# First 16 attention units: value product with queries on partitions, and x divided by the sums of its rows

## The chip, the cores and the metric

The kernel runs on one core of a Trainium2 chip. The metric is the device time of one execution in microseconds. A second source is the profile of one execution: a trace of every instruction of the five engines (PE is TensorE with its weight loads PEld, DVE is VectorE, ACT is ScalarE, POOL is GpSimd, SP is SyncE, which issues the transfers here), read as rows of several views.

## The reference

Attention with a bias from a running sum, then two feed-forward layers:

```
scores = q @ k.T / 8 + min(-(cum_i - cum_j), 0)     # causal, cum = cumsum(max(s, 0)); B=4, H=8, S=576, D=64
attn   = exp(scores - max) ; attn = attn / (sum(attn) + 1e-9)
x      = (attn @ v), heads side by side             # 2304 x 512
x      = (sigmoid(x @ w_gate) * (x @ w_val)) @ w_out  # 512 -> 1536 -> 512
h      = x @ w_in ; out = (h - tanh(h)) @ w_out2      # 512 -> 2048 -> 512
```

All inputs are fp32.

## The kernel before

Attention runs over 64 units, each one head of one batch with a group of queries: first the 256 leading queries (G = 0) of every batch and head, then the other 320 (G = 1). A unit of G = 0 has two steps, one for each tile of 128 queries (128 and 256 keys). The first N32 = 16 units (batches 0 and 1, steps 0 to 31) work in plain fp32; later ones split every operand in a high and a low part. The change is about these first 32 steps.

One loop over the steps writes the order of all engines out by hand; each engine works its instructions off in that order. In step i the loop issues, for the first 16 units:

- DVE: `ttr(i)`, the scaled scores and their minimum out of PSUM; then, for step i - 2, `eps` (adds 1e-9 to the row sum) and `recip`; `norm(i - 2)`, which multiplies the 128 x 128 or 128 x 256 tile of exponentials by the reciprocal, on POOL, from unit 13 on (steps 26 to 31) on DVE.
- ACT: `evac(i - 3)` (copies transposed probabilities out of PSUM), then `exp(i)` with the row sum as accumulator output.
- PE: the scores of step i + 2 (`qk`), a gate or value product of the feed-forward layer where there is one (`moe`, 12 matmuls of 256 columns) or, in the first 20 steps, a few warming products, then the transposes of step i - 2 (`tr`), then, every second step, a value product (`pv`), then a further gate or value product where two are due.
- the evacuation of the value product one step later (`xsum`): ACT writes the high part of x, and DVE the low part another step later (list `late`).

The value product has v of two heads as its stationary operand (128 columns: two heads of 64) and the transposed probabilities as the moving one, so x comes out with the head dimension on partitions, as the feed-forward layer wants it; of the two heads in the result only the unit's own half is read. Transposes go to PSUM banks 6 and 2 in turn for the first 16 steps, then to bank 6; the value product goes to bank 7; the gate products use banks 0 to 2, the scores 3 to 5.

When the last head of a batch has been written to x (`whole`), its 24 gate and value products are put into a queue `mq`. Each step takes as many as keep pace with the steps that are left:

```
k = -(-len(mq) // left) if i < n else 1
left -= 1
for mm in mq[:k]:
    cvt.finish(min(2 * mm[1] + mm[2] + AHEAD, len(cq) - 1))
```

The weights of these products come as 64-bit words and are turned into high and low fp32 parts on the way, 24 jobs in all. A tick of this conversion is one instruction on ACT (`words_scale`, L78), two on DVE for the job before (`words_join`, L82 and L83), and ACT's high part (L124) and POOL's low part (L114) for the job before that. There is a tick every third step up to step 15, one in each step from 18 on, and further ones where a product would come before its weights (`cvt.finish`).

Transfers are all issued by SP in the order of the loop: q and k of a unit four units ahead (`load_kq`, five buffers), its row of running sums (`load_sum`), v of a pair of heads two units ahead (`load_vc`, four buffers), weights by the conversion. A transfer whose buffer isn't free holds up those behind it.

Of the kernel before, what the change touches and what calls it, by code (L numbers as in the profile page):

```python
# [8 lines left out]
F = mybir.dt.float32  # L9
# [3 lines left out]
AF = mybir.ActivationFunctionType  # L13
ALU = mybir.AluOpType

B, H, S, D = 4, 8, 576, 64
# [14 lines left out]
NK = 4  # L31
# [6 lines left out]
N32 = 16  # L38
AHEAD = 1
TR2 = 16  # L40
# [18 lines left out]
def NORM(G, t):  # L59
    return "pool" if t > 2 else "dve"  # L60
# [3 lines left out]
def attention_moe_moe2(ctx: ExitStack, tc: tile.TileContext, kqT, v, s, wg, wv, wo, win, wo2, out):  # L64
# [8 lines left out]
    def bank(i, shape):  # L73
        return psum.tile(shape, F, tag=f"bank{i}", name=f"bank{i}")
# [205 lines left out]
    def load_vc(u):  # L280
        if u >= len(units):
            return
        b, h, q0, kw, qw, nj = shape(u)
        d = U_[u]
        if u < N32:
            if h % 2:
                d["v"] = U_[u - 1]["v"]
            else:
                d["v"] = at.tile([128, 2, 2, D], F, tag="kl", name="vpair", bufs=NK)
                for a in range(2):  # L290
                    SP.dma_start(out=d["v"][:, :, a], in_=v[b, h + a, :, 0:nj])
            return
        load_c(u)
        load_v(u)
# [138 lines left out]

    def exp(i):
        e = T_[i]
        e["sum"] = sm.tile([128, 1], F, tag="sum", name="sum")
        ACT.activation(out=e["sp"], in_=e["sp"], func=AF.Exp, scale=-1.0, bias=e["m"], accum_out=e["sum"])  # L437

    def eps(i):
        if 0 <= i < n:  # L440
            DVE.tensor_scalar(out=T_[i]["sum"], in0=T_[i]["sum"], scalar1=1e-9, scalar2=None, op0=ALU.add)

    def recip(i):
        if 0 <= i < n:
            T_[i]["r"] = sm.tile([128, 1], F, tag="r", name="r")
            DVE.reciprocal(out=T_[i]["r"], in_=T_[i]["sum"])

    def norm(i):
        if 0 <= i < n:
            e = T_[i]  # L450
            u, t = steps[i]
            if u < N32 - 3 or NORM(units[u][1], t) == "pool":
                POOL.tensor_scalar(out=e["sp"], in0=e["sp"], scalar1=e["r"], scalar2=1.0, op0=ALU.mult, op1=ALU.mult)  # L453
            else:
                DVE.tensor_scalar(out=e["sp"], in0=e["sp"], scalar1=e["r"], scalar2=None, op0=ALU.mult)

    def tr(i):
        if i < 0 or i >= len(steps):
            return
        u, t = steps[i]  # L460
        e = T_[i]
        blocks = [128 * j for j in range(t + 1)] if t < 4 else [0, 128, 256, 384, 448]
        ps = bank(2 if i < TR2 and i % 2 else 6, [128, min(len(blocks), 4), 128])
        e["tr"] = [ps]
        if t == 4:
            e["tr"].append(bank(3 + nqk[0] % 3, [128, 1, 128]))
            nqk[0] += 1
        for j, c in enumerate(blocks):
            PE.transpose(e["tr"][j // 4][:, j % 4, :], e["sp"][:, c:c + 128], ident)  # L469
# [24 lines left out]
        DVE.tensor_tensor(out=pl[:, js, o:o + 128], in0=tr0, in1=ph[:, js, o:o + 128].bitcast(F), op=ALU.subtract)  # L494

    X_ = {}
    late = []

    def pv(u):
        b, G, h = units[u]  # L500
        q0, qw, ts = GRP[G]
        d = U_.pop(u)
        ps = bank(7, [128, qw])
        if u < N32:
            for j in range(2):
                PE.matmul(ps[:, j * 128:], d["v"][:, j].rearrange("p a d -> p (a d)"),
                          d["p"][:, 2 * j:2].rearrange("p s q -> p (s q)") if j == 0 else d["p"][:, 2],
                          start=(j == 0), stop=(j == 1))
            return ps
        ph, pl = (P_[x][:, u % 2] for x in range(2))  # L510
        jobs = [(0, 0, 0), (1, 3, 0)] if G == 0 else [(0, 0, 0), (1, 1, 0), (2, 2, 0), (3, 3, 64), (4, 4, 64)]
        for n, (j, slot, o) in enumerate(jobs):
            for m, p in enumerate((ph, pl)):
                PE.matmul(ps[:, o:qw], d["vs"][:, j].rearrange("p a d -> p (a d)"), p[:, slot, o:qw],  # L514
                          start=(n == 0 and m == 0), stop=(n == len(jobs) - 1 and m == 1))
        return ps

    def xsum(u, ps):
        b, G, h = units[u]
        q0, qw, ts = GRP[G]  # L520
        g = 2 * b + G
        if h == 0:
            X_[g] = [xt.tile([128, KD, 320], R, tag=f"x{p}", name=f"x{p}")[:, :, :qw] for p in "hl"]
        a = 64 * (h % 2)
        if u < N32:
            xh, xl = (x[a:a + 64, h // 2, :] for x in X_[g])
            ACT.activation(out=xh, in_=ps[a:a + 64], func=AF.Copy)

            def rest():
                DVE.tensor_tensor(out=xl, in0=ps[a:a + 64], in1=xh.bitcast(F), op=ALU.subtract)  # L530

            if h == H - 1:
                rest()
            else:
                late.append(rest)
            return
        if h % 2 == 0:
            X_["pair"] = at.tile([128, 320], F, tag="xp", name="xp", bufs=1)[:, :qw]
        xp = X_["pair"]
        ACT.activation(out=xp[a:a + 64], in_=ps[64 - a:128 - a], func=AF.Copy)  # L540
        DVE.tensor_tensor(out=xp[a:a + 64], in0=ps[a:a + 64], in1=xp[a:a + 64], op=ALU.add)

    def xsplit(u):
        b, G, h = units[u]
        g = 2 * b + G
        if u >= N32 and h % 2:
            xp = X_["pair"]
            xh, xl = X_[g]
            ACT.activation(out=xh[:, h // 2, :], in_=xp, func=AF.Copy)
            POOL.tensor_tensor(out=xl[:, h // 2, :], in0=xp, in1=xh[:, h // 2, :].bitcast(F), op=ALU.subtract)  # L550
# [44 lines left out]
    SP.dma_start(out=sraw, in_=s.rearrange("b h s -> (b h) s"))  # L595
    kq32 = [ld.tile([65, 512], F, tag="kq", name=f"kq32{j}") for j in range(2)]
    kq32 += [at.tile([65, 512], F, tag="kh", name=f"kq32{j + 2}", bufs=NK) for j in range(NK - 1)]
    cvt = Conversion(cv, cq, 3, 3, 1, pt, 2, late=2, cut=2)
    for u in range(2):
        load_kq(u)  # L600
# [22 lines left out]
        DVE.tensor_tensor_scan(out=cum[:, c], data0=sraw[:, c], data1=zt[:, c], initial=init, op0=ALU.add, op1=ALU.add)  # L623
    load_sum(0)
    load_sum(1)
    for kq in ones[2:]:
        DVE.memset(kq, 1.0)
    cvt.load(2)
    load_vc(0)
# [19 lines left out]
    mq = []  # L649
    n = len(steps)  # L650
    lag = [2 if j < 2 * N32 else LN for j in range(n)]
    xq, xs, pvs = [], [], []

    def whole(xu):
        if units[xu][2] == H - 1 and xu < len(units) - 1:
            gg = 2 * units[xu][0] + units[xu][1]
            mq.extend((gg, m, w) for m in range(M1) for w in range(2))

    for i in range(n + LN + 2):
# [18 lines left out]
            recip(j)  # L678
            norm(j)
        cvt.low()  # L680
        while late:
            late.pop(0)()
        for e in es:
            evac(e)
        if i < n:
# [10 lines left out]
        while xq:  # L696
            xu, ps = xq.pop(0)
            xsum(xu, ps)
            if xu < N32:
                whole(xu)  # L700
            else:
                xs.append(xu)
        if first and vparts:
            vparts.pop(0)()
# [34 lines left out]
            warm(4 if i < 4 else 1)  # L739
        for j in js:  # L740
            tr(j)
        for e in es:
            if steps[e][1] in (1, 4):
                pvs.extend(range(steps[e][0] - steps[e][1] // 4, steps[e][0] + 1))
# [327 lines left out]
```

## Time and profile before

| | |
|---|---|
| time, median of 3 runs | 1058.3 us (1056.79 to 1058.71) |
| the profiled execution | 1059.05 us |
| its span, first to last instruction | 1057.3 us |
| PE busy | 1024.0 us, 97% |
| DVE, ACT, POOL busy | 629.3, 512.6, 457.3 us |
| mean granted clock of PE | 0.993 |
| steps 0 to 31 | from 7.6 to 92.0 us of the span |

The profiled execution is 0.75 us above the median. Times in the rows below count from the first instruction of the profiled execution. Where a row ends in square brackets, they hold how long the engine stood idle before it and what released it; the releaser is inferred.

### The profile page before, as it was taken

How to read it: one execution, taken by the hardware profiler on the slowest of the kernel's cores; microseconds unless marked ns; L12 is line 12 of the kernel's file. 1: busy time of each engine (PE TensorE's matmuls, PEld its weight loads, DVE VectorE, ACT ScalarE, POOL GpSimd, SP SyncE). 2: the span in 40 equal slices, each digit the busy share in tenths (PEclk: the TensorE clock that was granted, in tenths of full speed). 3: DMA queues.
4: the chain of work that ended last, by engine and by line, in shares of the span. 5: the costliest groups of instructions: out<-in, count | busy, mean ns of one | idle time of the engine just before them, and what ended most of it. 6: DMA issues, size and time to landing. Idle time of an engine off the chain costs nothing.

```text
span 1057.3 us, 19634 instructions
## 1 busy us (share of the span) xinstructions
PE 1024.0 (97%) x6812; PEld 952.9 (90%) x6812; DVE 629.3 (60%) x1467; ACT 512.6 (48%) x1178; POOL 457.3 (43%) x608
## 2 busy tenths in 40 slices
PE   6888999999999999999999999999999999999998
PEld 5687999999999999999988888988888889999997
DVE  5688565677576476644523544265755245877876
ACT  5776465677566566644423333244453233334333
POOL 3677454666557466623300100046555202454442
PEclk8999999999999999999999999999999999999999
DMA  6674456756565456316453332355687686444433
GB/s 190 215 238 126 116 139 166 205 148 181 154 176 171 135 180 185 111 43 220 159 166 112 119 119 77 116 177 204 233 294 288 244 311 237 147 114 140 140 98 103
DMA packets 109091, 177.09 MB, mean 167 GB/s; under 512 B 16000, under 2 KB 71296, under 8 KB 107712
## 3 DMA queue, kind: packets, MB, share of 16 engines
q1 hardware_dynamic: 108992, 175.85, 53.4%
q8 instruction: 53, 0.87, 0.3%
q14 instruction: 46, 0.38, 0.1%
HBM read 128.79 MB, written 47.00 MB: 166 GB/s over the span
## 4 chain that ended last, share of the span: by engine, by line
PE 83%; DMA 4%; POOL 3%; DVE 3%; ACT 3%; issue 3%; SPq 1%; POOLq 0%; DVEq 0%; ACTq 0%
PE bank L572 8%; PE bank L576 8%; PE bank L573 8%; PE bank L886 6%; PE bank L885 6%; PE bank L889 6%; PE bank L1025 5%; PE bank L1024 5%; PE bank L1023 5%; PE bank L847 5%; PE bank L843 5%; PE bank L844 5%; PE bank L514 4%; PE bank L469 4%; PE bank L410 1%
## 5 line engine op out<-in xcount | busy, mean ns | idle before, releaser
L1025 PE MATMUL bank<-wo,sl 128*128 128x256 f32 x504 | 142.9, 284 | 1.4 <-DVE sl L934 1.4
L1023 PE MATMUL bank<-wo,sh 128*128 128x256 f32 x504 | 141.7, 281 | 0.0
L1024 PE MATMUL bank<-wo,sh 128*128 128x256 f32 x504 | 141.7, 281 | 0.0
L886 PE MATMUL bank<-y,ring 128*128 128x512 f32 (+1 forms) x320 | 115.8, 368 | 0.0
L885 PE MATMUL bank<-y,ring 128*128 128x512 f32 (+1 forms) x320 | 115.7, 368 | 0.0
L892 DVE TENSOR_TENSOR th<-bank,th 128x512 f32<-128x512 f32 (+1 forms) x80 | 50.1, 635 | 92.3 <-ACT th L891 90.2
L114 POOL TENSOR_TENSOR ring<-tmp,ring 128x512 fp32r<-128x512 f32 x16 | 22.6, 1413 | 186.9 <-ACT ring L124 166.7
L493 ACT ACTIVATE pth<-bank 128x384 fp32r<-128x384 f32 (+1 forms) x96 | 45.4, 473 | 118.7 <-PE bank L469 93.2
L1025 PEld LDWEIGHTS bank<-wo,sl 128*128 128x128 f32 x504 | 95.2, 189 | 3.0 <-DVE sl L934 2.0
L929 POOL TENSOR_TENSOR s<-g 128x256 f32<-128x256 f32 (+1 forms) x40 | 36.9, 922 | 139.8 <-DMA g<-h 131.0
L494 DVE TENSOR_TENSOR ptl<-bank,pth 128x384 fp32r<-128x384 f32 (+1 forms) x96 | 51.2, 534 | 75.2 <-ACT pth L493 63.1
L1023 PEld LDWEIGHTS bank<-wo,sh 128*128 128x128 f32 x504 | 95.2, 189 | 0.0
L1024 PEld LDWEIGHTS bank<-wo,sh 128*128 128x128 f32 x504 | 95.2, 189 | 0.0
L800 DVE TENSOR_TENSOR gl<-g,gh 128x512 fp32r<-128x512 f32 (+1 forms) x60 | 37.8, 637 | 84.1 <-PE bank L847 62.5
L437 ACT ACTIVATE sp<-sp,nm 128x128 f32<-128x128 f32 (+4 forms) x144 | 83.5, 580 | 7.6 <-DVE nm L430 7.6
L469 PE MATMUL bank<-ident,sp 128*128 128x128 f32 x400 | 69.1, 277 | 16.8 <-POOL sp L453 6.6
L891 ACT ACTIVATE th<-bank 128x512 f32<-128x512 f32 (+1 forms) x80 | 43.5, 550 | 78.4 <-PE bank L889 75.8
L889 PE MATMUL bank<-y,ring 128*128 128x512 f32 (+1 forms) x320 | 78.7, 368 | 0.0
L799 ACT ACTIVATE gh<-g 128x512 fp32r<-128x512 f32 (+1 forms) x60 | 35.1, 591 | 90.0 <-PE bank L844 82.4
L588 DVE SCALAR_TENSOR_TENSOR gt<-th,bank 128x256 f32<-128x256 f32 (+1 forms) x96 | 43.2, 450 | 56.4 <-PE bank L576 41.9
L341 POOL TENSOR_TENSOR kl<-kq,kh 128x576 fp32r<-128x576 f32 (+1 forms) x48 | 57.7, 1203 | 38.9 <-ACT kh L340 38.5
L932 ACT ACTIVATE sh<-g 128x768 fp32r<-128x768 f32 (+1 forms) x40 | 31.2, 781 | 87.6 <-PE bank L1024 60.7
(385 smaller groups left out, 3181.3 us busy)
## 6 DMA issues: line engine op xcount, KB each, us to landing
h<-th SPq DMA_DIRECT2D x64, 256.0 KB, 2.7
kq<-in_kq SPq DMA_DIRECT2D x32, 448.0 KB, 3.6
raw<-in_wo SPq DMA_DIRECT2D x28, 512.0 KB, 4.7
g<-g SPq DMA_DIRECT2D x48, 256.0 KB, 2.7
g<-h SPq DMA_DIRECT2D x72, 128.0 KB, 2.2
w<-wst SPq DMA_DIRECT2D x5, 1792.0 KB, 6.6
wo<-w SPq DMA_DIRECT2D x5, 1792.0 KB, 9.1
cbc<-cum SPq DMA_DIRECT2D x32, 256.0 KB, 5.3
```

The lines of the kernel that those rows point to most:

```text
L341: POOL.tensor_tensor(out=kl, in0=d["k"], in1=kh.bitcast(F), op=ALU.subtract)
L437: ACT.activation(out=e["sp"], in_=e["sp"], func=AF.Exp, scale=-1.0, bias=e["m"], accum_out=e["sum"])
L469: PE.transpose(e["tr"][j // 4][:, j % 4, :], e["sp"][:, c:c + 128], ident)
L572: PE.matmul(ps, wh[:, c], xh[:, k], start=(k == 0), stop=False)
L573: PE.matmul(ps, wl[:, c], xh[:, k], start=False, stop=False)
L576: PE.matmul(ps, wh[:, c], xl[:, k], start=False, stop=(k == KD - 1))
L885: PE.matmul(ps, wh[:, c], yh[k], start=(k == 0), stop=False)
L886: PE.matmul(ps, wl[:, c], yh[k], start=False, stop=False)
L889: PE.matmul(ps, wh[:, c], yl[k], start=False, stop=(k == KD - 1))
L1023: PE.matmul(o, sh[:, g, c], w[:, 0, f], start=(p == 0 and t == 0), stop=False)
L1024: PE.matmul(o, sh[:, g, c], w[:, 1, f], start=False, stop=False)
L1025: PE.matmul(o, sl[:, g, c], w[:, 0, f], start=False, stop=(p == MP - 1 and t == nt - 1))
```

## The change

For the first 16 units the probabilities are no longer divided before the value product. The exponentials go to the transposes as they are, and `exp` no longer asks for the row sum, so that `eps`, `recip` and `norm` fall away there. The value product is turned round: the transposed exponentials (128 keys x 128 queries) are stationary and v with a 65th column of ones moves, so that the result has the queries on partitions, 64 columns of x and in the 65th the row sum: three matmuls of 65 columns for a unit instead of two of 256 and 128. For a pair of heads DVE adds the epsilon to the four sums of each partition, takes their reciprocals and multiplies x by them into SBUF (`xsum`, tile xq); PE transposes it back to the head dimension on partitions (`xturn`, two transposes for the pair, into the second half of bank 6), and one step later ACT and DVE write the high and the low part of x for both heads at once (`xsplit`). A batch is whole one step later than before.

v has three buffers of its own (places of tiles that are used later) with the column of ones set once at the start; transposes and the return share bank 6 as one tile for its whole use.

```diff
-                d["v"] = at.tile([128, 2, 2, D], F, tag="kl", name="vpair", bufs=NK)
+                d["v"] = v32[u // 2 % 3]
                 for a in range(2):
-                    SP.dma_start(out=d["v"][:, :, a], in_=v[b, h + a, :, 0:nj])
+                    SP.dma_start(out=d["v"][:, :, a, 0:D], in_=v[b, h + a, :, 0:nj])
...
     def exp(i):
         e = T_[i]
+        if steps[i][0] < N32:
+            ACT.activation(out=e["sp"], in_=e["sp"], func=AF.Exp, scale=-1.0, bias=e["m"])
+            return
...
     def eps(i):
-        if 0 <= i < n:
+        if 2 * N32 <= i < n:
...
     def recip(i):
-        if 0 <= i < n:
+        if 2 * N32 <= i < n:
...
     def norm(i):
-        if 0 <= i < n:
+        if 2 * N32 <= i < n:
...
-            if u < N32 - 3 or NORM(units[u][1], t) == "pool":
+            if NORM(units[u][1], t) == "pool":
...
-        ps = bank(2 if i < TR2 and i % 2 else 6, [128, min(len(blocks), 4), 128])
+        if u < N32 + 2:
+            o = 256 * (i == 2 * N32)
+            ps = E_[i < TR2 and i % 2][:, o:o + 128 * (t + 1)].rearrange("p (j q) -> p j q", q=128)
+        else:
+            ps = bank(6, [128, min(len(blocks), 4), 128])
...
     def pv(u):
+        if u < N32:
+            a = h % 2
+            if a == 0:
+                X_["pv"] = bank(7, [128, 2, 2, D + 1])
+            ps = X_["pv"]
+            PE.matmul(ps[:, 0, a], d["p"][:, 0], d["v"][:, 0, a], start=True, stop=True)
+            PE.matmul(ps[:, 1, a], d["p"][:, 1], d["v"][:, 0, a], start=True, stop=False)
+            PE.matmul(ps[:, 1, a], d["p"][:, 2], d["v"][:, 1, a], start=False, stop=True)
+            return ps
         ps = bank(7, [128, qw])
-        if u < N32:
-            for j in range(2):
-                PE.matmul(ps[:, j * 128:], d["v"][:, j].rearrange("p a d -> p (a d)"),
-                          d["p"][:, 2 * j:2].rearrange("p s q -> p (s q)") if j == 0 else d["p"][:, 2],
-                          start=(j == 0), stop=(j == 1))
-            return ps
...
         if u < N32:
-            xh, xl = (x[a:a + 64, h // 2, :] for x in X_[g])
-            ACT.activation(out=xh, in_=ps[a:a + 64], func=AF.Copy)
-
-            def rest():
-                DVE.tensor_tensor(out=xl, in0=ps[a:a + 64], in1=xh.bitcast(F), op=ALU.subtract)
-
-            if h == H - 1:
-                rest()
-            else:
-                late.append(rest)
+            if a:
+                z, r = (sm.tile([128, 2, 2], F, tag=k, name=k) for k in ("z4", "r4"))
+                xq = X_["q"] = at.tile([128, 2, 2, D], F, tag="xp", name="xq", bufs=1)
+                DVE.tensor_scalar(out=z, in0=ps[:, :, :, D], scalar1=1e-9, scalar2=None, op0=ALU.add)
+                DVE.reciprocal(out=r, in_=z)
+                DVE.tensor_tensor(out=xq, in0=ps[:, :, :, 0:D], in1=r.unsqueeze(3).broadcast_to([128, 2, 2, D]),
+                                  op=ALU.mult)
+                xr.append(u)
             return
...
+    def xturn(u):
+        for t in range(2):
+            PE.transpose(E_[0][:, 256 + 128 * t:384 + 128 * t], X_["q"][:, t].rearrange("p a d -> p (a d)"), ident)
+        xs.append(u)
+
     def xsplit(u):
         b, G, h = units[u]
         g = 2 * b + G
-        if u >= N32 and h % 2:
+        if u < N32:
+            xh, xl = (x[:, h // 2, :] for x in X_[g])
+            ACT.activation(out=xh, in_=E_[0][:, 256:512], func=AF.Copy)
+            DVE.tensor_tensor(out=xl, in0=E_[0][:, 256:512], in1=xh.bitcast(F), op=ALU.subtract)
+        elif h % 2:
...
+    c4s = ld.tile([128, 2, 2, 2, D + 1], F, tag="c4", name="v32", bufs=1)
+    v32 = [c4s[:, 0], c4s[:, 1], ld.tile([128, 2, 2, D + 1], F, tag="v", name="v32b")]
+    E_ = [bank(6, [128, 512]), bank(2, [128, 512])]
...
-    for kq in ones[2:]:
+    for kq in ones[2:] + [vt[:, :, :, D] for vt in v32]:
         DVE.memset(kq, 1.0)
...
-        while late:
-            late.pop(0)()
...
             xsum(xu, ps)
-            if xu < N32:
-                whole(xu)
-            else:
+            if xu >= N32:
                 xs.append(xu)
...
         for j in js:
             tr(j)
+        while xr:
+            xturn(xr.pop(0))
```

## Rows read from the trace of the kernel before

**Rows 1.** The page's slices (40 of 26.4 us), busy tenths of PE.

```profile
PE   6888999999999999999999999999999999999998
```

**Rows 2.** Windows: length, busy PE, PEld, DVE, ACT, POOL (instructions), granted clock, transfers.

```profile
20.40:27.30 6.90, 6.65 (x31) 5.47 (x29) 4.16 (x20) 4.11 (x14) 1.33 (x3) 0.61 0.63 178
27.30:44.00 16.70, 12.95 (x86) 10.33 (x86) 11.67 (x47) 14.03 (x45) 10.07 (x19) 1.00 0.80 247
...
62.20:77.70 15.50, 13.93 (x110) 12.96 (x108) 13.59 (x30) 11.10 (x27) 11.94 (x16) 1.00 0.81 262
77.70:92.00 14.30, 11.70 (x78) 11.05 (x78) 12.96 (x35) 10.34 (x30) 11.57 (x19) 0.88 0.43 122
92.00:102.20 10.20, 7.35 (x52) 6.26 (x51) 7.49 (x32) 6.66 (x24) 8.74 (x17) 1.00 0.45 117
```

**Rows 3.** Timeline, 27 to 46 us: transposes that wait, and a scaling on POOL.

```profile
27.96 0.33 PE L469 MATMUL bank<-ident,sp 128*128 128x128 f32 x1 [0.92 <-POOL sp L453]
...
36.58 0.38 POOL L453 TENSOR_SCALAR sp<-sp,r 128x128 f32<-128x128 f32 x1
37.01 0.33 PE L469 MATMUL bank<-ident,sp 128*128 128x128 f32 x1 [1.20 <-DMA vpair<-in_v]
...
41.57 0.44 PE L469 MATMUL bank<-ident,sp 128*128 128x128 f32 x2 [0.65 <-POOL sp L453]
45.13 0.33 PE L469 MATMUL bank<-ident,sp 128*128 128x128 f32 x1 [1.36 <-POOL sp L453]
```

**Rows 4.** Timeline of DVE: starts of steps 21, 24, 28, 30, 32.

```profile
45.54 0.41 DVE L430 CUSTOM_DVE_ANT_0 sp<-bank,consts 128x256 f32<-128x256 f32 x1
...
57.06 0.28 DVE L430 CUSTOM_DVE_ANT_0 sp<-bank,consts 128x128 f32<-128x128 f32 x1
...
77.68 0.28 DVE L430 CUSTOM_DVE_ANT_0 sp<-bank,consts 128x128 f32<-128x128 f32 x1
...
86.11 0.29 DVE L430 CUSTOM_DVE_ANT_0 sp<-bank,consts 128x128 f32<-128x128 f32 x1 [0.26 <-PE bank L469]
...
92.01 0.28 DVE L430 CUSTOM_DVE_ANT_0 sp<-bank,cbc 128x128 f32<-128x128 f32 x1
```

**Rows 5.** Timeline of step 28: scaling on DVE, transpose, value product.

```profile
78.27 1.19 DVE L455 TENSOR_SCALAR sp<-sp,r 128x128 f32<-128x128 f32 x1
...
79.61 0.30 PE L469 MATMUL bank<-ident,sp 128*128 128x128 f32 x1 [1.90 <-ACT qs L345]
...
79.97 1.32 PE L506 MATMUL bank<-p,vpair 128*128 128x256 f32 x4
```

**Rows 6.** Timeline of PE: a value product, one transpose, two transposes.

```profile
28.13 0.82 PE L506 MATMUL bank<-p,vpair 128*128 128x256 f32 x4
...
30.00 0.27 PE L469 MATMUL bank<-ident,sp 128*128 128x128 f32 x1
...
35.04 0.38 PE L469 MATMUL bank<-ident,sp 128*128 128x128 f32 x2
```

**Rows 7.** The chain that ended last, in order of time.

```profile
13.14 6.12 DMA kq<-cumsum
```

**Rows 8.** Groups by line and shape, 0 to 110 us: busy us, mean ns.

```profile
L437 ACT ACTIVATION_READ_ACCUMULATOR sp<-sp,nm 128x1 f32 x39 | 7.4, 190 | 0.0
...
L530 DVE TENSOR_TENSOR xl<-bank,xh 64x256 fp32r<-64x256 f32 x16 | 6.7, 419 | 6.3 <-ACT xh L527 5.9
...
L453 POOL TENSOR_SCALAR sp<-sp,r 128x256 f32<-128x256 f32 x13 | 6.3, 483 | 6.5 <-DVE r L446 6.0 <-ACT sp L437 0.3
...
L446 DVE RECIPROCAL r<-sum 128x1 f32<-128x1 f32 x38 | 6.2, 162 | 1.9 <-DVE sum L441 0.5
...
L441 DVE TENSOR_SCALAR sum<-sum 128x1 f32<-128x1 f32 x38 | 5.5, 147 | 0.7 <-ACT sp L437 0.6
```

**Rows 9.** Timeline of step 25: a gate product's evacuation on DVE.

```profile
63.53 0.42 DVE L588 SCALAR_TENSOR_TENSOR gt<-th,bank 128x256 f32<-128x256 f32 x1 [0.67 <-ACT th L585]
```

**Rows 10.** Timeline of SP's queue: the load of v for pair 4.

```profile
27.22 1.09 SPq L291 DMA_DIRECT2D vpair<-in_v  x2
```

More of the change, by code (lines that the diff above doesn't have):

```diff
@@ L496, in attention_moe_moe2 @@
     X_ = {}
-    late = []
     def pv(u):
@@ L651, in attention_moe_moe2 @@
     lag = [2 if j < 2 * N32 else LN for j in range(n)]
-    xq, xs, pvs = [], [], []
+    xq, xs, xr, pvs = [], [], [], []
     def whole(xu):
```

## Prediction

> **What bounds the kernel now.** The change touches only the first 32 steps of the attention loop (16 units of two steps each) and what hangs on them, so I first looked in the page's slices and then in the windows for where that stage ends and whether TensorE (PE) is full there. From the fifth slice on (a slice is 26 us) PE is busy nine tenths or more to the end [rows 1], so a microsecond won or lost earlier reaches the end of the kernel nearly whole. Inside the stage PE is not full: it is busy 12.95 of 16.7 us in steps 12 to 20, 13.93 of 15.5 in steps 25 to 28, 11.70 of 14.3 in steps 28 to 32, and 7.35 of 10.2 in steps 32 to 36 [rows 2]. I then read PE's own waits in the timeline. Five transposes between 27 and 44 us wait for the scaled probabilities (the normalisation, L453 on POOL): 0.92, 0.80, 0.21, 1.20 and 0.65, together 3.8 us, and a sixth at 45.13 waits 1.36 [rows 3] (the second and the third are of the pattern of the first). The wait at 37.01 is put down to the load of v; that is misread, since the load that it names serves a later pair, while POOL's scaling of the very tile ends at 36.58 + 0.38 = 36.96 [rows 3]. So the loop now is: DVE's reduction, epsilon, reciprocal, POOL's scaling, PE's transpose.
>
> In steps 24 to 28 the picture is another: 57.06 to 77.68 is 20.6 us for four steps, 5.2 us each, against 11.5 us for the three steps before (45.54 to 57.06, 3.84 each) [rows 4], and DVE is busy 13.59 of 15.5 us in the later three [rows 2]. There the join of the weight words on DVE sets the pace (two conversion ticks in a step), and PE waits for weights and queue, not for attention. The expensive spot is step 28: the scaling of a 128x128 tile on DVE takes 1.19 us, PE waits 1.90 us for it, and the next value product runs at 1.32 us where it takes 0.82 elsewhere [rows 5, 6]; the granted clock of 77.7 to 92 is 0.88 [rows 2], that is, between PE's two levels, with the lower one right behind this wait.
>
> **Before step 8: nothing.** The score product that PE issues in step 6 waits for a load that was issued at 13.14 and took 6.12 us [rows 7]; the change leaves the order of these loads alone. The three new memsets of the column of ones lie ahead of that, behind the same wait.
>
> **PE's own work (B).** Before, a value product is four passes over 256, 256, 128 and 128 columns: 0.82 us from first start to last end [rows 6], about 0.64 without the last one's latency. After, it is three products of 65 columns, six passes, each with its own load of 128 columns. Two neighbouring transposes, each a load and 128 columns, take 0.38 us where one takes 0.27 [rows 6], so 0.11 a pass; at half the columns a pass costs between 0.055 and 0.11, six of them 0.33 to 0.66. I take 0.66, no gain, because each still loads 128 columns and that row is the nearest. New are two transposes for a pair, 0.22. By the Trainium skill ("TensorE: Matmul & The Clock Gate", LDWEIGHTS and the section on the weight-path modes) a load's time goes with its columns, about 107 ns for 128, and fp32 weights get no fast load: by that rule shorter streams bring nothing here; without it PE would gain some 0.3 us a unit, 5 us over 16 units of PE work, of which only the part where PE is the bound counts. The trace of before can't separate load from stream, as no pass in it has fewer columns than it loads. From 20.4 to 27.3 the granted clock is 0.61 and PE is the bound, 6.65 of 6.9 us [rows 2]: one return of a pair falls there at about twice its price, **+0.4** (from -1.5, if six passes cost half, to +0.6).
>
> **The normalisation leaves the chain, steps 12 to 20 (C).** Out go epsilon (147 ns) and reciprocal (162) in each step, the accumulator read on ACT (190) and the scaling on POOL (483 for 256 columns) [rows 8]. A transpose then waits for the exponential of two steps earlier, which is long done. The 3.8 us of waits go. Against that, for three pairs: the return transposes 0.22 each (0.7), and a new wait. PE's return stands in its queue behind the step's own transpose and waits for DVE's epsilon, reciprocal and division of the pair: 0.15 + 0.16 + 0.42 (the division by the nearest row, the subtraction of 256 columns out of PSUM, L530 [rows 8]) plus latencies, about 1.1 us after the value product ends, against some 0.75 of scores, warming products and transposes that PE has in between (an estimate: 0.4 + 0.1 + 0.22): 0.35 a pair, 1.0 in all. Queued behind it: the next score product of DVE's chain. Sum -3.8 + 0.7 + 1.0 = **-2.1** (0 to -3.8).
>
> **The wait at 45.13 (D1)** is of the same kind, behind a join on DVE: **-1.4** (0 to -1.4).
>
> **A batch's gate and value products start one step later (D2, F).** x is now split a step after it is formed, so the products of batch 0 start in step 21, not 20, those of batch 1 in 37, not 36. By the loop's own rule (jobs left over steps left) steps 20 to 31 then lose two steps with one product and get one with two and an empty one. Two steps with one product cost 5.90 us (86.11 to 92.01); one with two costs 3.84 [rows 4]; an empty one I take at the mean of steps 12 to 20, 16.7/8 = 2.1 [rows 2]: 5.9 against 5.9, **0** (-1.0 to +1.2). In step 36 there is no such trade: PE stands while the step runs, and the products are made up later where PE is full. A step there is 10.2/4 = 2.55 us [rows 2], PE's own work in it about 1.0 (an estimate, the scores, transposes and half a value product): **+1.5** (0 to +2.5).
>
> **Steps paced by DVE (D3).** Here the removed DVE work is mostly worth nothing: DVE waits 0.67 us for ACT's tanh before the gate product even with epsilon and reciprocal in front of it [rows 9], as that tanh stands behind the step's exponential. Only ACT's shorter exponential (about 0.1 a step, five steps, -0.5) counts. New on DVE, once in these steps: the pair's division, 0.75, and the low part of x, which now stands ahead of the gate product and waits for ACT's high part, 0.4. **+0.7** (-0.4 to +1.5). DVE's 0.42 a unit for the old low part goes, but it fitted into the same gap.
>
> **Step 28 (E).** Scaling on DVE disappears. PE's wait of 1.90 and the lower clock behind it (0.12 of 14.3 us, 1.7) are the most that can come back, 3.6. DVE still has the joins; I take what the scaling with its two small operations holds DVE up, 1.5, and half of the clock's loss: **-2.4** (0 to -3.6).
>
> **Loads.** v has three buffers for pairs where it had four. The load for pair 4 was issued at 27.22; its buffer would now be free when unit 3's value product ends, 28.13 + 0.82 = 28.95 [rows 6, 10]. SP then stands 1.7 us, with two loads of q, k and one of weights behind it. They are due some seven steps later, at 2.1 us a step, against the 6.1 us of the slowest load seen [rows 7]: hidden. Were steps to fall to about 1 us, a score product would wait for what is then missing, at most the 1.7 us that SP stood. The v rows of 260 bytes move the same 256-byte pieces: nothing.
>
> **Sum.** +0.4 - 2.1 - 1.4 + 0 + 1.5 + 0.7 - 2.4 = -3.3 us. The profiled execution took 1059.05 us (span 1057.3), so 1055.75; it lies 0.75 above the median of the runs shown, 1058.3, for which this gives **1055.0**.
>
> **Rivals.** *No change that can be measured* (within 0.2%, 2.1 us): the conversion on DVE sets the end of steps 20 to 32 whatever attention does, so D1 and E fall out, and the -2.1 of C is given back in step 36. For it: DVE's 13.59 of 15.5 us; against it: PE's 1.90 in step 28 ends on the scaling, not on a join. 0.4 - 2.1 + 1.5 + 0.7 = +0.5: 1058.8. Chance 0.28. *The return makes it slower*: DVE comes to the pair's division behind joins or behind the gate product, and PE stands at the return 1.4 us instead of 0.35, with the second product of the step behind it. Three pairs of C then cost 3 x 1.05 more and two pairs in the product steps 2 x 1.4: +6.0 on the forecast, +2.7, 1061. It decides against the change from about 1 us of wait a pair. For it: the same order of DVE now holds PE up at 45.13; against it: three of four steps have no such wait at all, where now each has one. Chance 0.15. *All waits go*: C at -3.8, D1, E at -3.6, and the shorter passes show in B (-1.5) with F at +1.5 and D3 at 0: -8.8, 1049.5. Chance 0.10. *The clock* is a small one inside these: step 20 has neither warming products nor gate products now; if PE falls to its lower level there, as it did behind 79.6, it costs the same 1.7 us again.
>
> **How the numbers follow.** The forecast, a gain of 2.1 to 6 us, has 0.47; with the case in which all waits go, faster by over 0.2% has 0.57, within 0.28, slower 0.15. 0.2% is about what a measurement of this kernel can tell from none. The range 1051 to 1060.5 holds the forecast's bounds (C, E and F at one end each) and the no-change case; the two outer cases are left out with about 0.2 between them. For the forecast alone it is 1052.3 to 1056.2.
>
> **What would show it.** Right: no transpose in the first 32 steps waits for POOL; PE's waits stand at the returns, about 0.35 us, in every fourth step; step 20 reached some 2 us earlier; no 1.9 us gap in step 28 and a clock of 1.0 there; the batch-1 products one step later with PE idle in step 36. Wrong: returns that wait over 1 us; six passes taking clearly less than 0.66 us, or more; the steps around 60 to 80 us as long as before and longer by the division; SP standing at v with a score product waiting for its load.

## The result and the profile after

Medians: 1057.55 us before (1055.25 to 1058.71, 4 runs) and 1066.31 us after (1066.05 to 1067.82, 4 runs). The ratio is 1.0093, 95% interval [1.0075, 1.0111]: slower by 0.9% (the two medians alone differ by 8.8 us), where 1055.0 was forecast, and above the range's end of 1060.5. The profiled execution after took 1066.05 us, its span is 1064.3 (before: 1059.05 and 1057.3), so about 7 us are to be found in the two traces.

The page of the kernel after, busy tenths of PE and the granted clock in 40 slices of 26.6 us; the first line answers to [rows 1]:

```profile
PE   7998899999999999999999999999999999999998
...
PEclk8599999999999999999999999999999999999999
```

The second digit of the clock is 5: in the slice from 27 to 53 us the granted clock is 0.50, TensorE's lower level, 1.2 GHz, throughout. The windows of the kernel after, one for each stage, answer to [rows 2] (columns as there); the windows begin at steps 8, 12, 20, 24, 28 and 32:

```profile
20.96:29.65 8.69, 8.37 (x38) 7.14 (x37) 3.40 (x15) 4.05 (x11) 1.41 (x2) 0.50 0.60 177
29.65:49.07 19.42, 18.21 (x81) 15.76 (x80) 10.10 (x33) 10.41 (x27) 6.45 (x8) 0.50 0.53 158
49.07:64.08 15.01, 13.91 (x94) 13.01 (x94) 8.67 (x23) 8.06 (x19) 7.07 (x9) 0.77 0.58 173
64.08:81.37 17.29, 17.29 (x146) 16.96 (x146) 12.14 (x29) 10.71 (x25) 8.86 (x11) 1.00 0.76 241
81.37:99.03 17.66, 15.15 (x117) 13.79 (x117) 14.13 (x30) 12.20 (x30) 16.24 (x24) 1.00 0.65 179
99.03:108.93 9.90, 6.90 (x56) 6.30 (x54) 5.42 (x27) 6.04 (x22) 8.26 (x16) 1.00 0.35 109
```

Read the clock column first. In steps 12 to 20 it is 0.50 where it was 1.00 [rows 2], PE is busy 18.21 of 19.42 us instead of 12.95 of 16.70, and DVE's share has fallen: PE has become the bound of the stage by running at half speed, not by having more to do. In windows of 0.1 us the lower level lasts from 18.4 to 55.9 us, 37.5 us; before it was 18.9 to 25.8 and 80.4 to 83.8.

What PE waits for in these steps, from the view of waits of the kernel after, 0 to 120 us (us in total, times, longest), and one row of SP's queue:

```profile
PE bank L476 <- DVE xl L561: 3.6, 6, 1.1
...
PE bank L552 <- DVE xq L540: 0.7, 1, 0.7
...
SPq L291 <- PE bank L516: 12.8, 6, 3.4
```

L476 is the transpose of the probabilities, L552 the return of the divided pair, L561 the low part of x. The returns hardly wait for the division (0.7 once); six transposes wait for the low part of x. The timeline of the kernel after around step 16 shows why:

```profile
40.14 0.40 ACT L437 ACTIVATE sp<-sp,nm 128x128 f32<-128x128 f32 x1 [0.45 <-DVE nm L430]
40.44 0.36 ACT L560 ACTIVATE xh<-bank 128x256 fp32r<-128x256 f32 x1
...
40.84 0.42 DVE L561 TENSOR_TENSOR xl<-bank,xh 128x256 fp32r<-128x256 f32 x1 [0.74 <-ACT xh L560]
...
41.32 0.48 PE L476 MATMUL bank<-ident,sp 128*128 128x128 f32 x1 [0.88 <-DVE xl L561]
```

The return writes the second half of bank 6, the even steps' transposes write the first half of the same tile (`E_[0]`, o = 0 and 256). So the transpose of step 14, ready long before, waits until the returned pair has been read by ACT (behind this step's exponential) and by DVE: 0.88 us here, 1.10 at the most. The transposes no longer wait for POOL, as forecast; they wait for this instead of [rows 3].

How long each stretch of steps takes in the profiled executions, in us, by the starts of the steps' minima in DVE's timelines. The last two columns are experiments told below: the change with a bank of its own for the return and more warming products, and the kernel before without its division.

| steps | before | after | own bank, warming | before, no division |
|---|---|---|---|---|
| to 8 | 20.42 | 20.96 | 21.02 | 18.70 |
| 8 to 12 | 6.91 | 8.69 | 6.72 | 5.61 |
| 12 to 20 | 16.62 | 19.42 | 14.31 | 15.23 |
| 20 to 32 | 48.06 | 49.96 | 45.68 | 41.97 |
| 32 to 36 | 10.21 | 9.90 | 9.91 | 10.90 |
| 36 to 50 | 41.43 | 44.21 | 43.72 | 41.42 |

After is 9.5 us behind at step 50 and 9.6 at the end of attention (461.39 against 471.00); 2.6 us come back behind it: in the kernel before PE waited 1.9 us for a tanh and the clock was at the lower level behind that wait (486.5 to 490 us); in the kernel after it waits 0.8 us and the clock stays up. The windows from 480 to 500 us, before (clock 0.91) and then after (1.00), show that part; after is some 9.6 us behind in them, so they don't hold quite the same work:

```profile
480.00:500.00 20.00, 18.09 (x113) 17.82 (x112) 8.69 (x16) 8.70 (x17) 5.58 (x5) 0.91 0.78 258
```

```profile
480.00:500.00 20.00, 19.22 (x133) 18.95 (x132) 7.31 (x12) 6.82 (x14) 3.89 (x3) 1.00 0.51 169
```

### The profile page after: what moved, and what is told of

Read it like the earlier page. It is cut to its first block, busy times and chain, and to the rows that moved or that the text cites. A ratio compares the mean times of both kernels' runs of the same rounds, so it can differ in the third digit from the quotient of the medians.

```text
span 1064.3 us, 19579 instructions
## 1 busy us (share of the span) xinstructions
PE 1037.6 (97%) x6860; PEld 965.7 (91%) x6860; DVE 622.0 (58%) x1416; ACT 506.6 (48%) x1138; POOL 447.8 (42%) x582
## 4 chain that ended last, share of the span: by engine, by line
PE 80%; POOL 3%; ACT 2%; issue 2%; DVE 2%; DMA 1%; SPq 0%; POOLq 0%; DVEq 0%; ACTq 0%
PE bank L588 7%; PE bank L589 7%; PE bank L592 7%; PE bank L903 6%; PE bank L902 6%; PE bank L906 6%; PE bank L1042 5%; PE bank L1040 5%; PE bank L1041 5%; PE bank L861 5%; PE bank L864 5%; PE bank L860 5%; PE bank L523 4%; PE bank L476 3%; PE bank L410 1%
## 5 line engine op out<-in xcount | busy, mean ns | idle before, releaser
L476 PE MATMUL bank<-ident,sp 128*128 128x128 f32 x400 | 71.6, 284 | 12.1 <-DVE ptl L501 5.0
L903 PEld LDWEIGHTS bank<-y,ring 128*128 128x128 f32 x320 | 60.3, 189 | 10.1
```

What stands on the lines that cost most here:

```text
L903: PE.matmul(ps, wl[:, c], yh[k], start=False, stop=False)
```

## The experiments

Ratios are to the kernel before on the same chip (medians 1056.35, 1054.89, 1057.06 and 1055.94 us in the four groups of runs), with 95% intervals. Single executions of these variants scatter by 2 to 10 us, so a profiled execution is told with its time.

### The wait or the clock: four variants of the change

**e1_more_warm**: more warming products in steps 4 to 19; their results are used by nothing.

```
-            warm(4 if i < 4 else 1)
+            warm(4 if i < 4 else 3)
```

> After, with three warming products (256 columns, bf16) instead of one in steps 4 to 19. In after the granted clock stays at its lower level from 18 to 53 us though PE is busy nearly throughout. Theory 1 (the short value product keeps the clock down: its passes wait for their loads and stream only 65 columns, so the array does too little): with more streamed columns in these steps the clock comes back before 35 us and step 20 is reached at 40 to 45 us instead of 49; about 1060 us. Theory 2 (the clock stays down because PE stops at every return and transpose for DVE): the stops stay, the clock stays down until the gate products begin, and the added products cost time at the lower clock: 1067 to 1070 us. Theory 3 (the clock matters little, the order of work costs the time): the clock may come back, the time stays within 2 us of after, 1066.

1063.49 us (1058.18 to 1065.12, 10 runs), 1.0055 [1.0038, 1.0072]. **e2_wide_stream**: each value pass streams 128 columns instead of 65, out of the pair's tile; both heads of a pair then stream the same columns, and the second head's own are left out.

```
-                X_["pv"] = bank(7, [128, 2, 2, D + 1])
+                X_["pv"] = bank(7, [128, 2, 2, 128])
...
+            v0, v1 = (d["v"][:, j].rearrange("p a d -> p (a d)")[:, 0:128] for j in range(2))
```

> After, with 128 columns of v of both heads streamed in each of the six passes instead of 65 (the sums of one of the two heads and part of the results are not the reference's; number of passes, loads, DVE and ACT work are those of after). Theory 1 (too few streamed columns hold the clock down): a pass takes as long as before, 0.11 us at full and 0.21 at half clock, since the load of 128 columns sets it, and the clock comes back before 35 us; 1058 to 1063 us. Theory 2 (stops): no change, clock down to 53 us, 1066. Theory 3: clock may come back, 1066.

1059.89 us (1054.46 to 1064.25, 8 runs), 1.0037 [1.0013, 1.0062]. **e3_own_bank**: the return gets a bank that no transpose uses: bank 1 for the first four pairs, then one of the three score banks.

```
+        if u < 8:
+            ps = bank(1, [128, 256])
+        else:
+            ps = bank(3 + nqk[0] % 3, [128, 256])
+            nqk[0] += 1
...
-            PE.transpose(E_[0][:, 256 + 128 * t:384 + 128 * t], ...
+            PE.transpose(ps[:, 128 * t:128 * t + 128], ...
...
```

> After, with the return of x in a PSUM bank of its own (bank 1, from pair 4 on one of the score banks) instead of the second half of the transposes' bank. In after six transposes wait 3.6 us in all for the low part of x, which is read from the other half of that bank. Theory 2 (stops hold the clock down): these waits go, the clock comes back earlier than 53 us, 1058 to 1062. Theory 1 (columns): the waits go but the clock stays down up to the first gate products; 1 to 3 us less than after, 1063 to 1065. Theory 3: 3 to 4 us less than after from the waits alone, 1062 to 1063.

1056.19 us (1052.47 to 1059.94, 10 runs), 0.9996 [0.9976, 1.0017]: with this alone no loss is left that can be measured. **e4_bridge**: 22 warming products once, at the end of step 5.

```
+        if i == 5:
+            warm(22)
```

> After, with 22 warming products (about 2.4 us) at the end of step 5, where PE stands 2.45 us for the load of q and k, behind which the clock falls. Theories 1 and 2 (the lower clock from 18 to 53 us costs the time): if the clock does not fall there, step 20 is reached near 40 us and the whole takes 1056 to 1061; if it falls all the same a little later, nothing changes, 1066. Theory 3 (order of work): clock full, time within 2 us of after.

1059.12 us (1057.48 to 1060.95, 10 runs), 1.0019 [1.0004, 1.0035]. Its profiled execution (1060.95, the slowest of its runs) goes through steps 8 to 15 at full clock and loses it in the course of one wait, a row of its timeline of PE:

```profile
36.68 0.48 PE L476 MATMUL bank<-ident,sp 128*128 128x128 f32 x1 [2.49 <-DMA v32b<-in_v]
```

The releaser is misread, as in [rows 3]: L561, the low part of x, ends at 36.63 there. From 36 to 53 us the clock is then at the lower level.

What follows. Three edits that leave the shared bank and its waits in place, and only give PE more to do (e1, e2, e4), win 4 to 8 us: the clock is a large part of the loss, and theory 3, by which it matters little, doesn't hold. One edit that takes the shared bank away wins 10 us, and the clock comes back with it: in e3 it rises at 25 us, as before, with one more stretch at the lower level from 38 to 48. So theories 1 and 2 each hold in part.

The granted clock, averaged over the execution, is on record for every run, and it parts the two. By and large the slower runs of one kernel are those with the lower clock: e1 goes from 1058.18 us at 0.995 to 1065.12 at 0.985, and after's four runs lie at 0.978 to 0.981. At the same mean clock of 0.992, six runs of e1, e2 and e4 take 1057.9 to 1060.7 us and two of e3 1056.8 and 1057.1. An estimate from these few runs: 2 to 3 us of the loss are the shared bank's waits by themselves, and some 7 come with the clock, which those waits hold down.

Both show in one window from 18 to 56 us, of e1 (profiled at 1058.18, its fastest run), then of e3 (1057.06), then of e5 (1052.96), told next; after has 35.36 busy at clock 0.51 there.

```profile
18.00:56.00 38.00, 32.07 (x236) 28.53 (x237) 21.94 (x69) 22.73 (x58) 14.11 (x18) 0.91 0.61 192
```

```profile
18.00:56.00 38.00, 35.02 (x220) 31.86 (x221) 23.11 (x72) 22.45 (x59) 15.26 (x20) 0.78 0.63 198
```

```profile
18.00:56.00 38.00, 35.41 (x277) 32.16 (x278) 25.48 (x77) 24.86 (x64) 16.60 (x21) 0.96 0.68 214
```

In e1's execution the waits for the low part of x are still there, 6.2 us in five, with the clock mostly high; so of the profiled times 1066.05, 1058.18 and 1052.96, the first step (7.9 us) is mostly the clock and the second (5.2) mostly the waits. The first is from e1's best run; six of its ten take 1063 to 1065 us, with a mean clock of 0.985 to 0.987 against 0.995, and at which wait the clock fell in them no trace shows.

### What the change is worth without the two

**e5_bank_warm** is e3 with e1's warming. **e7_before_warm** is the kernel before with the same warming, the fair one to set beside it.

> After with the return in a bank of its own and three warming products instead of one in steps 4 to 19. With the bank alone the time is that of before (1056.2 beside 1056.4), but the clock still falls for 6 us behind the start's load and for 10 us around step 19. Theory 1 (what is left over the forecast is the lower clock): both stretches get shorter, 1052 to 1054 us. Theory 2 (the conversion on DVE sets the end of the stage, the clock before step 20 costs nothing any more): no change against the bank alone, 1056 within 1.5 us.

> Before, with three warming products instead of one in steps 4 to 19: control for the clock. Theory 1 (the lower clock ahead of step 20 costs before some time too: 6.5 us at half clock, PE the bound there): 1 to 3 us less than before, 1053 to 1055. Theory 2: the added products stand in PE's queue ahead of the transposes, and time stays or grows, 1056 to 1058.

e5: 1053.32 us (1050.78 to 1055.95, 10 runs), 0.9979 [0.9962, 0.9995]. e7: 1053.16 us (1052.04 to 1055.81, 10 runs), 0.9986 [0.9971, 1.0001]. With bank and clock out of the way the change is worth nothing that can be measured. **e6_bank_same_step**: e3, but a batch's last pair is split in the step of its return, so that the gate products start in steps 20 and 36 as before.

```
+            if units[xu][2] == H - 1:
+                xs.pop()
+                xsplit(xu)
+                whole(xu)
```

> After with the return in a bank of its own, and the last pair of a batch split in the same step in which it is returned, so that the gate and value products of both batches start in step 20 and 36 as in before. Theory 1 (the later start leaves PE idle in step 36 and is made up later; +2.8 us between steps 36 and 50 in the profile of after, +1.2 with the bank alone): 1.5 to 2.5 us less than with the bank alone, 1053.7 to 1054.7. Theory 2 (an empty step costs nothing, since the conversion sets the pace): within 0.7 us of the bank alone.

1056.4 us (1054.98 to 1059.37, 10 runs), 1.0014 [0.9998, 1.0029], no gain over e3's 0.9996. In its profiled execution, the slowest of its runs, steps 36 to 50 take 42.28 us where e3 has 42.60, and steps 32 to 36 take 12.24 where e3 has 9.94. Its two returns of a batch's end wait 2.8 us for the division, and behind the first (1.99 us, at 75.25) the clock is at its lower level from 76 to 82 us: the earlier start gives hardly anything, and more is lost at another place. **e8_before_no_division**: the kernel before without sums, epsilon, reciprocal and scaling in the first 32 steps; the result is not divided there.

```
+        if steps[i][0] < N32:
+            ACT.activation(out=e["sp"], in_=e["sp"], func=AF.Exp, scale=-1.0, bias=e["m"])
+            return
...
-        if 0 <= i < n:
+        if 2 * N32 <= i < n:
...
```

> Before, with the sums, epsilon, reciprocal and scaling of the first 32 steps left out (the result is not divided) and nothing put in their place; value product as in before. The part of the change that the forecast priced at C + D1 + E. Theory 1 (transposes waiting for the scaled tile are on the path): 4 to 7 us less than before, 1049.5 to 1052.5. Theory 2 (the conversion on DVE sets the end of steps 20 to 32): at most 2 us less, 1054.5 to 1056.5.

1045.1 us (1044.38 to 1046.77, 4 runs), 0.99 [0.9874, 0.9927]: 9.8 us for what the change takes out. So the thing removed is worth more than the forecast gave it, and what is put in its place costs 1.0093 - 0.9900, about 20 us, of which 10 are the shared bank with the clock (e3); the warming on top of it takes off 2 more (e5), of which the kernel before gets 1.5 as well (e7).

### The remaining 8 us

**e9_bank_late_low**: e5, with the low part of a returned pair subtracted in the next step, behind the joins, as before. **e10_bank_no_division**: e5 with one copy in place of sums, reciprocal and multiplication; the result is not divided.

```
...
+            def rest():
+                DVE.tensor_tensor(out=xl, in0=xb, in1=xh.bitcast(F), op=ALU.subtract)
+            if h == H - 1:
+                rest()
+            else:
+                late.append(rest)
```

```
-                DVE.tensor_scalar(out=z, in0=ps[:, :, :, D], ...
-                DVE.reciprocal(out=r, in_=z)
-                DVE.tensor_tensor(out=xq, in0=ps[:, :, :, 0:D], ...
+                DVE.tensor_copy(out=xq, in_=ps[:, :, :, 0:D])
```

> The change with the return in a bank of its own and three warming products (0.9979 [0.9962, 0.9995] of before), and here the low part of a returned pair is subtracted in the next step, behind the joins, as the kernel before did, instead of right behind the high part. Theory 1: a part of the 8 us that separate that version from the kernel without any division is DVE standing 0.74 us for the high part of each pair, with the gate and the next minimum behind it; then eight pairs give 2 to 5 us: 1048 to 1051 against before at 1055, ratio 0.993 to 0.996. Rival: DVE would have stood for something else in that time anyway, and the rest is the longer work on PE and the division itself; then it stays at 0.998, within 0.0015.

> The same version with the pair's sums, reciprocal and multiplication left out: one copy of the product to SBUF stands in their place and the result is not divided. Theory 1: the division of a pair on DVE is on the path; three operations of 0.16, 0.18 and 0.43 us become one of about 0.4, so eight pairs give back 8 times 0.35 = 2.8 us, 1050, ratio 0.995. Rival 1: the division costs nothing and the way through the return (product, copy, transposes, split) is the whole of the 8 us: 0.998. Rival 2: the division holds up more than its own length, since PE's transposes wait for it: 1046 to 1048, ratio 0.991 to 0.993.

e9: 1053.52 us (1049.45 to 1058.06, 12 runs), 0.9963 [0.9944, 0.9982], the best version that still divides. e10: 1052.07 us (1050.02 to 1054.31, 6 runs), 0.9958 [0.9941, 0.9974]. Against e5's 0.9979 the later subtraction brings 1.7 us (less than the 2 to 5 expected) and the division on DVE costs 2.2, about the forecast of 2.8; e5's interval overlaps with both. DVE's wait for the high part falls from 6.6 us in e5 to 2.6 in e9, its wait for tanh rises from 6.2 to 9.7 (view of waits of DVE, 18 to 92 us, e5 first):

```profile
DVE xl L567 <- ACT xh L566: 6.6, 7, 1.7
DVE gt L610 <- ACT th L607: 6.2, 7, 1.1
```

```profile
DVE gt L619 <- ACT th L616: 9.7, 10, 1.5
...
DVE xl L571 <- ACT xh L568: 2.6, 3, 1.5
```

**e11_late_ring** and **e12_warm_ring**: e9 and e5 with bank 2 for the returns from the fifth pair on and two banks in place of three for the first batch's gate and value products, since in steps 20 to 32 of e5 PE's score product waits 2.6 us for DVE's minimum in the score banks that the return has joined.

```
-            ps = bank(3 + nqk[0] % 3, [128, 256])
+            ps = bank(2, [128, 256])
...
-        ps = bank(nmo[0] % 3, [128, qw])
+        ps = bank(nmo[0] % (2 if g == 0 else 3), [128, qw])
```

> The version with the return in a bank of its own, three warming products and the low part subtracted a step later (0.9963 [0.9944, 0.9982] of before). From the fifth pair on its return took one of the three score banks, and PE's score product then waited 2.4 us in all for DVE's minimum of the tile before. Here the return has bank 2 for itself in these pairs, and the gate and value products of the first batch turn over two banks instead of three. Theory 1: those waits are a part of what still separates this version from the kernel without any division; they go, and steps 20 to 32 get 2 to 2.5 us shorter: 0.994. Rival: two banks are too few, gate products wait for their evacuation behind tanh, and it is not faster: 0.996 to 0.999, with waits of PE for gt or th in place of the old ones.

> The same banks, in the version with three warming products and the low part subtracted at once (0.9979 [0.9962, 0.9995] of before; PE's score product waited 2.6 us in all for the minimum in steps 20 to 32). Theory 1: 2 to 2.5 us back, 0.9955. Rival: the two-bank ring takes it back, 0.998 to 1.000. Beside the other kernel of this call it also shows again, on one chip, what the later subtraction is worth: 0.0015 if the earlier pair of results holds, nothing if that was scatter.

e11: 1054.85 us (1051.39 to 1057.19, 12 runs), 0.9985 [0.9971, 1.0000]. e12: 1055.57 us (1052.69 to 1060.57, 12 runs), 1.0003 [0.9985, 1.0021]. The rival held. The two differ in the later subtraction alone, and it is again about 2 us better, again with intervals that overlap. PE's waits, 18 to 92 us in e9 and 18 to 112 us in e11:

```profile
PE bank L391 <- DVE nm L430: 2.4, 3, 1.1
```

```profile
PE bank L602 <- ACT th L615: 4.5, 4, 1.7
...
PE bank L391 <- DVE nm L430: 0.3, 1, 0.3
```

The wait for the minimum is gone and one for tanh (L602, a gate product that wants its bank back) has taken its place. All eight banks have a user, and the return has to sit in front of somebody.

## Why the prediction was wrong

**The step that failed** is in C: "A transpose then waits for the exponential of two steps earlier, which is long done." It follows the probabilities alone. The diff puts the return into the tile of bank 6 that the even steps' transposes write, so a transpose also waits for ACT and DVE to have read the returned pair. That was there to be read in two lines of the diff (`o = 256 * ...` in `tr`, `E_[0][:, 256 ...` in `xturn`). C was forecast at -2.1 us and steps 12 to 20 measured +2.8; with a bank of its own (e5 against e7, 14.31 and 16.00) they measure -1.7. So without the shared bank C's sum is near, but that is luck, as its terms weren't right: the removal was to give 3.8 us in these steps and gives 1.4 in e8 (15.23 for 16.62), and the return was to cost 1.7 and costs nothing in e5 (14.31 for e8's 15.23, with e5's warming, which gave the kernel before 0.6).

**The clock** failed with it. It stood as "a small one", 1.7 us, once. It was at the lower level for 37.5 us, and 7.9 us of the profiled time went when e1's best run had it high. The stage before the change already began at that level [rows 2]; the text asked only whether PE would fall back to it, not whether PE would still climb out.

**The slower rival** had the right suspect and the wrong end of it: PE was to stand ahead of the return, 1.4 us a pair; it stood 0.7 us once there, and up to 1.1 us behind it, at the next even step's transpose. Its +2.7 us had no clock in it.

**B held.** Two rows of the timeline of PE in the kernel after, a value product at full clock:

```profile
13.90 0.33 PE L514 MATMUL bank<-v,p 128*128 128x65 f32 x2
...
14.52 0.65 PE L391 MATMUL bank<-kq 65*128 65x256 f32 x2
```

And the same place in e2, with 128 columns in each pass:

```profile
13.70 0.39 PE L515 MATMUL bank<-v,p 128*128 128x128 f32 x2
...
14.37 0.60 PE L391 MATMUL bank<-kq 65*128 65x256 f32 x2
```

From 13.90 to the next product's start at 14.52 are 0.62 us for six passes, 0.10 each, against 0.66 taken; with 128 columns they are 0.67. So halving the streamed columns gives 0.05 us in six passes, and the load of 128 columns, the same in both, is left as what sets the time. This agrees with the Trainium skill ("TensorE: Matmul & The Clock Gate", "LDWEIGHTS (loading the stationary operand)"), by which a load goes with its columns. What B had wrong is the place: PE was taken as the bound at half clock only from 20.4 to 27.3; steps 8 to 12 measured +1.8 us for +0.4, and the stage stayed there.

**D3 was the wrong way round.** "The removed DVE work is mostly worth nothing" came from one tanh that DVE waits for [rows 9]. Without the division steps 20 to 32 take 41.97 us instead of 48.06 (windows of e8 and, for e5, of the same steps):

```profile
39.54:81.51 41.97, 40.22 (x316) 38.28 (x315) 33.03 (x71) 31.60 (x75) 31.41 (x40) 1.00 0.74 233
```

```profile
42.05:87.73 45.68, 42.54 (x348) 41.11 (x348) 34.91 (x79) 30.43 (x72) 33.06 (x43) 1.00 0.68 216
```

That is -6.1 us, where D1 and E together were -3.8: epsilon, reciprocal and scaling in every step were worth some 2 us more than the forecast gave them. In turn the cost of what is put there, +0.7 net of ACT's shorter exponential, was too small: e5 gets 3.7 us less than e8, and still has the pair's division (e10: 2.2 us in the whole kernel).

**D1, D2, E** can't be told apart in the totals. Forecast for steps 20 to 32 with D3: -3.1. Measured: +1.9 in after, -1.8 in e5 against e7 (47.48). E's place did change as said, two rows of PE's timeline in the kernel after at step 28 (compare [rows 5]):

```profile
82.97 0.33 PE L476 MATMUL bank<-ident,sp 128*128 128x128 f32 x1 [0.31 <-DVE xl L561]
83.13 0.34 PE L514 MATMUL bank<-v,p 128*128 128x65 f32 x2
```

0.31 us of wait instead of 1.90, and the clock is 1.00 in that window instead of 0.88. Steps 28 to 32 are 3.3 us longer all the same (17.66), with 117 records of PE where before had 78: more of the gate and value products, which start later, fall into them.

**F isn't confirmed.** Steps 32 to 50 take 2.5 us more after (-0.3 and +2.8) for the +1.5, but only 0.9 more in e3 than before and 0.5 more in e5 than in e7, and e6, which takes the later start away, doesn't shorten them. How much of the 2.5 us is the later start is open.

**Loads were right in the outcome, not in the size:** SP stood at the v loads 12.8 us in six waits, not 1.7 once, and still the last score product that waits for its load (2.45 us) starts at 18.01, ahead of SP's long stands, which begin at 25.05.

**Before step 8** was to change nothing. Counted from the score product that waits for its load, step 8's minimum starts 2.95 us behind it in the kernel after (18.01 to 20.96) and 1.02 in the kernel before (19.40 to 20.42), 2.36 in e5 and 0.66 in e7. Two rows of DVE's timeline in the kernel after show why:

```profile
20.21 0.16 DVE L538 TENSOR_SCALAR z<-bank 128x4 f32<-128x4 f32 x1 [4.47 <-PE bank L516]
...
20.96 0.28 DVE L430 CUSTOM_DVE_ANT_0 sp<-bank,consts 128x128 f32<-128x128 f32 x1
```

The pair's epsilon (L538) stands in DVE's queue ahead of step 8's minimum (L430) and waits for a value product that PE reaches only behind the loaded scores. The forecast priced PE's wait for the division, and put DVE's own wait for the value product at nothing. It comes again at the next three pairs, 2.34 us each in after; in e5 it is 6.8 us in three.

**Still open:** from e10 (0.9958) to e8 (0.9900) are 6 us that the division doesn't explain, and the clock only in part (medians of the runs' mean clock 0.9945 and 0.997). Most of them lie in steps 20 to 32, 46.52 us in e10's profiled execution and 41.97 in e8's: PE is busy 3.2 us longer there (43.41 and 40.22) and waits 2.6 us for DVE's minimum, which it doesn't in e8. What is left in that place is the return's copy, transposes and split, the later start, a bank that is always somebody else's, and, in the first 20 steps, DVE's wait for the value product, which no run took away (6.3 us in three in e10). The trials with the bank and with the start moved the wait and won nothing, so what each is worth alone isn't settled.

## What to carry to other kernels

When a change puts a new result into half of a tile that another stage fills, list who must have read that half before the other stage may write again: here six waits of about 0.6 us, with the clock behind them, cost about 10 us, as much as the division that was removed. Where a stage starts at the lower clock with PE nearly full, price the case in which it never leaves it, since all of PE's further work is then paid at half speed. And price the removal alone before the replacement, by a run that leaves it out: here it was worth 9.8 us, and the way around it took them all.

## What the runs showed of the hardware

The lower clock can go with a PE that looks full. Windows of 10 us in the kernel after:

```profile
20.00:30.00 10.00, 9.68 (x42) 8.08 (x42) 4.38 (x19) 4.05 (x11) 1.41 (x2) 0.50 0.56 166
30.00:40.00 10.00, 9.68 (x44) 8.38 (x43) 5.15 (x15) 5.57 (x14) 3.58 (x4) 0.50 0.59 162
40.00:50.00 10.00, 8.59 (x38) 7.05 (x36) 4.95 (x18) 5.74 (x16) 3.54 (x4) 0.50 0.46 149
```

PE is busy 9.68 of 10 us in the first two and the granted clock is 0.50 in all three; it rises at 55.9 us, when the gate products run. The same program doesn't fall there every time in the same way: e1's ten runs lie between 1058.18 us (mean clock 0.995) and 1065.12 (0.985), e9's twelve between 1049.45 (0.997) and 1058.06 (0.991), while after's four, low for 37.5 us in the one that was profiled, lie within 1.8 us at 0.978 to 0.981.
